# A dense layer with squared ReLU: the four weight chunks of the opening stage on one column half before the other, and the requests reordered to match

## The chip, the cores and the metric

The kernel runs on one core of one Trainium2 chip. Its time is the device time in microseconds, the median of several runs. TensorE multiplies, VectorE and ScalarE copy and apply the activation, SyncE and ScalarE issue the transfers from memory.

## What is computed

```python
B, S, D, F = 1, 2048, 576, 4608          # bf16
h = einsum("bsd,df->bsf", x, w1) + b1
h = relu(h) ** 2
out = einsum("bsf,fd->bsd", h, w2) + b2
```

The inner dimension of the first product is D = 576 = 4 x 128 + 64. The kernel walks over x in four blocks of 512 rows, and over the 4608 columns of w1 in 36 tiles of 128.

## The kernel before

The first product needs x transposed. For blocks 1 to 3 a transposing transfer does it. For block 0, which cannot wait for that, x comes as it is, in four row tiles of 128 rows (`xs`), and TensorE transposes it by chunks of 128 columns. Column half 0 of the transposed block holds row tiles 0 and 1, half 1 holds row tiles 2 and 3. The first four column tiles of w1 (`qn`, "natural" chunks: 128 rows of w1 by 512 columns each) are used with 128-row matmuls, so that TensorE has something to do with few bytes landed. All other columns of w1 are laid out in 64-row pieces (`w1h`, two column tiles to a pair) and are multiplied with pairs of 64-row matmuls.

The requests, in the order of the program; the two issuing queues work side by side, each in its own order:

```python
    load_x(nc.sync, 0)
    load_x(nc.scalar, 1)
    load_quad(nc.sync, 0)
    load_quad(nc.scalar, 1)
    load_x(nc.sync, 2)
    load_x(nc.scalar, 3)
    load_quad(nc.sync, 2)
    load_quad(nc.scalar, 3)
    # ... one dummy activation
    for h in range(2):
        load_rest(nc.sync, h)           # last 64 rows of w1, 512 columns

    for j0, n in ((2, 1), (3, 1), (4, 1), (5, 1), (6, 2), (8, 2), (10, 2), (12, 2), (14, 2), (16, 2)):
        for h in range(2):
            load_w1(nc.sync, h, j0, n, slice(0, NH))     # n pairs from pair j0
```

The two helpers of the opening stage: transposes of some chunks of one half, each followed by a copy out of PSUM on the engine named (V for VectorE, A for ScalarE; chunk NC is the odd rest and takes two copies); and the four matmuls of one chunk on one half.

```python
    def transpose_chunks(half, cs, engs):
        tps = [psum.tile([P, HALF], BF16, name="tp", tag="bank") for c in cs]
        for i in range(2):
            for c, tp in zip(cs, tps):
                d0 = c * P if c < NC else D - P
                nc.tensor.transpose(tp[:, i * P:(i + 1) * P], xs[:, 2 * half + i, d0:d0 + P], ident[:])   # L167
        cols = slice(half * HALF, (half + 1) * HALF)
        for c, tp, eng in zip(cs, tps, engs):
            copy_psum(eng, xT[0][:, c if c < NC else 7, cols], tp[:])            # L160 VectorE, L158 ScalarE
            if c == NC:
                nc.vector.tensor_copy(out=xT[0][0:H, 8, cols], in_=tp[H:P, :])

    def full_mm(half, c):
        cols = slice(half * HALF, (half + 1) * HALF)
        for q in range(4):
            nc.tensor.matmul(bk0[q][:, cols], lhsT=qn[:, c, q * P:(q + 1) * P], rhs=xT[0][:, c, cols], ...)   # L213
```

And the stage itself, in TensorE's order:

```python
    transpose_chunks(0, (0,), (V,))
    transpose_chunks(0, (1,), (A,))
    fill(HALF)
    full_mm(0, 0)
    transpose_chunks(0, (2, NC), (A, V))
    full_mm(0, 1)
    transpose_chunks(0, (3,), (A,))
    transpose_chunks(1, (0, 1, 2), (V, A, V))
    full_mm(1, 0)
    transpose_chunks(1, (NC,), (V,))
    full_mm(1, 1)
    transpose_chunks(1, (3,), (A,))
    full_mm(0, 2)
    full_mm(1, 2)
    # ... transpose of the bias to b1T (L232)
    full_mm(0, 3)
    full_mm(1, 3)
    # ... four matmuls with the last 64 rows (L239), evacuation of the four banks
```

After it come the pairs 2 to 17 of block 0 (`a_step`, 18 matmuls of 64 rows by 512 columns to a pair, L198), then blocks 1 to 3 with all pairs, then the second product (L302, L316).

Of the kernel before, what the change touches and what calls it, by code (L numbers as in the profile page):

```python
# [17 lines left out]
def kernel(  # L18
# [9 lines left out]
    nc = tc.nc  # L28
# [10 lines left out]
    NC = D // P  # L39
# [51 lines left out]
    def load_x(eng, j):  # L91
        eng.dma_start(out=xs[:, j, :], in_=x_view[:, j, :])  # L92

    def load_quad(eng, c):
        eng.dma_start(out=qn[:, c, :], in_=w1[c * P:(c + 1) * P, 0:G * P])  # L95

    def load_w1(eng, h, j0, n, cs):
        f0 = pairs[j0][h] * P
        eng.dma_start(out=w1h[h * H:(h + 1) * H, cs, j0 * P:(j0 + n) * P], in_=w1_rows[:, cs, f0:f0 + n * P])
# [7 lines left out]
    load_x(nc.scalar, 1)  # L107
    load_quad(nc.sync, 0)
    load_quad(nc.scalar, 1)
    load_x(nc.sync, 2)  # L110
    load_x(nc.scalar, 3)
    load_quad(nc.sync, 2)
    load_quad(nc.scalar, 3)
    nc.scalar.activation(out=warm[:], in_=nc.const_aps.tensor(1.0, [P, 1], FP32), func=ACT.Relu)
    for h in range(2):
        load_rest(nc.sync, h)


    for j0, n in ((2, 1), (3, 1), (4, 1), (5, 1), (6, 2), (8, 2), (10, 2), (12, 2), (14, 2), (16, 2)):
        for h in range(2):  # L120
            load_w1(nc.sync, h, j0, n, slice(0, NH))

# [33 lines left out]
    def copy_psum(eng, dst, src):  # L156
        if eng is nc.scalar:
            nc.scalar.copy(out=dst, in_=src)  # L158
        else:
            nc.vector.tensor_copy(out=dst, in_=src)  # L160
# [9 lines that stand above are left out]
            copy_psum(eng, xT[0][:, c if c < NC else 7, cols], tp[:])  # L170
            if c == NC:
                nc.vector.tensor_copy(out=xT[0][0:H, 8, cols], in_=tp[H:P, :])
# [37 lines left out]
# [3 lines that stand above are left out]
            nc.tensor.matmul(bk0[q][:, cols], lhsT=qn[:, c, q * P:(q + 1) * P], rhs=xT[0][:, c, cols],  # L213
                             start=(half == 0 and c == 0), stop=False, skip_group_check=True)

    V, A = nc.vector, nc.scalar
# [4 lines left out]
    transpose_chunks(0, (2, NC), (A, V))  # L221
    full_mm(0, 1)
    transpose_chunks(0, (3,), (A,))
    transpose_chunks(1, (0, 1, 2), (V, A, V))
    full_mm(1, 0)
    transpose_chunks(1, (NC,), (V,))
    full_mm(1, 1)
    transpose_chunks(1, (3,), (A,))
    full_mm(0, 2)
    full_mm(1, 2)  # L230
    b1T_ps = psum.tile([P, P], BF16, name="b1T_ps", tag="bank")
    nc.tensor.transpose(b1T_ps[:], b1_rows[:], ident[:])  # L232
    nc.vector.tensor_copy(out=b1T[:], in_=b1T_ps[:, 0:NFT])
    full_mm(0, 3)
    full_mm(1, 3)
    for i in range(2):
        for h in range(2):
# [118 lines left out]
```

## Time and profile before

| what | value |
|---|---|
| time, median of 3 runs | 291.2 us (290.83 to 291.26) |
| span of the profiled execution | 289.1 us |
| granted TensorE clock, mean | 1.0 of full speed |
| first transpose on TensorE | 2.87 us |
| first pair (L198) on TensorE | 9.76 us |
| w1 pairs, 22 loads by SyncE | 3.3 to 7.8 us from issue to landing |

The profile is of one execution. Its times start at the span's beginning. PE is TensorE's matmuls, PEld its weight loads, DVE is VectorE, ACT is ScalarE; SPq and ACTq are the queues in which SyncE and ScalarE issue transfers. A line such as L167 is a line of the kernel. In the names of the program, `w_sb` covers the several buffers that share the later home of w2: xs, the transposed x and the natural chunks of w1 among them; x is told from w1 there by what is read, `in_x_dram` or `in_w_dram`.

### The profile page before, as it was taken

The page shows a single profiled execution, that of the slowest core. Times are in us where ns is not written, and L with a number is a line of the kernel's source. Part 1 is how long each engine was busy: PE and PEld are TensorE (multiplying, and loading weights), DVE is VectorE, ACT ScalarE, POOL GpSimd, SP SyncE. Part 2 cuts the span into 40 slices and gives each one's busy share as a digit, 9 for nine tenths or more (in the row PEclk, how much of TensorE's full clock was granted, in tenths as well). Part 3 has the DMA queues.
Part 4 walks back from the last instruction along what each step waited for, and adds up shares of the span by engine and source line. Part 5 has one row for each costly group of instructions (what it writes and reads, how often), then busy time and mean ns, then how long its engine had stood idle before and what let it go on. Part 6 is the DMA issues. An engine that isn't in the chain of part 4 may idle for free.

```text
span 289.1 us, 4823 instructions
## 1 busy us (share of the span) xinstructions
PE 284.3 (98%) x2068; PEld 133.3 (46%) x2079; DVE 79.2 (27%) x195; ACT 95.4 (33%) x153; POOL 1.5 (1%) x8
## 2 busy tenths in 40 slices
PE   8999999999999999999999999999999999999995
PEld 5544444444444444444445444444444444444454
DVE  2644454444445444444420011111100011111111
ACT  3666666666666666666620000000000000000000
POOL 2000000000000000000000000000000000000000
PEclk9999999999999999999999999999999999999999
DMA  7999998800300006100000100000000000000000
GB/s 202 210 232 197 212 184 195 299 0 2 120 5 2 1 2 207 40 0 2 0 2 19 20 20 20 20 23 11 10 20 23 20 20 20 24 20 20 20 23 20
DMA packets 35413, 18.01 MB, mean 62 GB/s; under 512 B 19380, under 2 KB 35392, under 8 KB 35392
## 3 DMA queue, kind: packets, MB, share of 16 engines
q1 hardware_dynamic: 34784, 17.14, 25.5%
q10 hardware_dynamic: 576, 0.56, 0.6%
q8 instruction: 16, 0.26, 0.4%
q14 instruction: 5, 0.04, 0.0%
q0 software_dynamic: 32, 0.01, 0.0%
HBM read 11.94 MB, written 2.36 MB: 49 GB/s over the span
## 4 chain that ended last, share of the span: by engine, by line
PE 97%; DMA 2%; issue 0%; SPq 0%; DVE 0%
PE ph L198 47%; PE po L316 43%; PE pc L302 5%; DMA w_sb<-in_x_dram 2%; PE ph L213 1%; PE tp L167 0%; PE ph L239 0%; SPq L95 0%; SPq L92 0%; DVE w_sb L160 0%; DVE o_sb L318 0%; PE b1T_ps L232 0%; SPq L340 0%
## 5 line engine op out<-in xcount | busy, mean ns | idle before, releaser
L182 ACT ACTIVATE r<-ph,b1T 128x512 bf16<-128x512 f32 x144 | 90.8, 684 | 48.4 <-PE ph L198 46.6
L198 PE MATMUL ph<-w_sb,w1h 64*128 64x512 bf16 x936 | 101.2, 376 | 0.0
L198 PEld LDWEIGHTS <-w1h 64*128 64x128 bf16 x1260 | 61.3, 94 | 74.7
L316 PE MATMUL po<-w_sb,hT 128*128 128x512 bf16 x423 | 92.9, 379 | 0.5
L316 PEld LDWEIGHTS <-hT 128*128 128x128 bf16 x432 | 42.2, 98 | 51.1 <-issue 0.4
L184 DVE TENSOR_TENSOR hT<-r 128x512 bf16<-128x512 bf16 x108 | 45.9, 425 | 54.8 <-ACT r L182 54.1
L318 DVE TENSOR_TENSOR o_sb<-po,b_bc 128x512 bf16<-128x512 f32 (+2 forms) x17 | 11.2, 660 | 116.7 <-PE po L316 109.7
L198 PE MATMUL ph<-xT,w1h 64*128 64x512 bf16 x324 | 35.1, 376 | 0.0
L316 PE MATMUL po<-w_sb,w1h 128*128 128x512 bf16 (+2 forms) x178 | 31.2, 336 | 0.1
L316 PEld LDWEIGHTS <-w1h 128*128 128x128 bf16 x180 | 16.2, 98 | 15.3
L184 DVE TENSOR_TENSOR w1h<-r 128x512 bf16<-128x512 bf16 x36 | 15.3, 425 | 19.7 <-ACT r L182 19.5
L302 PE MATMUL pc<-hT,w_sb 128*64 128x512 bf16 x108 | 15.7, 379 | 0.0
L302 PEld LDWEIGHTS <-w_sb 128*64 128x64 bf16 x144 | 8.1, 110 | 7.6 <-issue 0.4
L302 PE MATMUL pc<-w1h,w_sb 128*64 128x512 bf16 x36 | 7.9, 379 | 0.0
L304 ACT ACTIVATE oc<-pc,b2T 128x512 bf16<-128x512 f32 x2 | 1.4, 687 | 13.7 <-PE pc L302 13.7
L312 DVE COPY o_sb<-oc 128x64 bf16<-128x64 bf16 x16 | 2.7, 171 | 9.3 <-DMA oc<-oc 9.3
L213 PE MATMUL ph<-w_sb 128*128 128x256 bf16 x32 | 4.5, 283 | 0.3 <-DVE w_sb L160 0.3
L213 PEld LDWEIGHTS <-w_sb 128*128 128x128 bf16 x32 | 3.1, 103 | 1.0 <-issue 0.6
L150 PE MATMUL wps<-const-bfloat16-1.0 128*128 128x512 bf16 x5 | 2.3, 624 | 0.8 <-PEq L340 0.8
L160 DVE COPY w_sb<-tp 128x256 bf16<-128x256 bf16 x5 | 1.4, 289 | 5.7 <-PE tp L167 5.7
L158 ACT COPY w_sb<-tp 128x256 bf16<-128x256 bf16 x5 | 1.8, 368 | 2.6 <-PE tp L167 2.6
L167 PE MATMUL tp<-ident,w_sb 128*128 128x128 bf16 x20 | 2.5, 239 | 0.1
(28 smaller groups left out, 11.2 us busy)
## 6 DMA issues: line engine op xcount, KB each, us to landing
w_sb<-in_w_dram SPq DMA_DIRECT2D x6, 864.0 KB, 7.1
w1h<-in_w_dram SPq DMA_DIRECT2D x14, 288.0 KB, 7.1
out_dram<-o_sb SPq DMA_DIRECT2D x15, 144.0 KB, 1.7
w1h<-in_w_dram SPq DMA_DIRECT2D x8, 144.0 KB, 3.6
w_sb<-in_x_dram SPq DMA_DIRECT2D x2, 144.0 KB, 3.3
w_sb<-in_x_dram ACTq DMA_DIRECT2D x2, 144.0 KB, 3.5
w_sb<-in_w_dram SPq DMA_DIRECT2D x2, 128.0 KB, 3.7
w_sb<-in_w_dram ACTq DMA_DIRECT2D x2, 128.0 KB, 3.9
```

What stands on the lines that cost most here:

```text
L150: nc.tensor.matmul(wps[:], lhsT=ones[:, 0:P], rhs=ones[:], start=(i == 0), stop=(i == NWARM - 1))
L158: nc.scalar.copy(out=dst, in_=src)
L160: nc.vector.tensor_copy(out=dst, in_=src)
L167: nc.tensor.transpose(tp[:, i * P:(i + 1) * P], xs[:, 2 * half + i, d0:d0 + P], ident[:])
L182: nc.scalar.activation(out=r[:], in_=bk[:], func=ACT.Relu, bias=b1T[:, ft:ft + 1], scale=1.0)
L184: nc.vector.tensor_tensor(out=hT_of(b, ft), in0=r3, in1=r3, op=ALU.mult)
L198: nc.tensor.matmul(bk[h][:], lhsT=w1h[rows, c, j * P:(j + 1) * P], rhs=xT[b][rows, place(h, c), :], start=(i == 0), stop=(i == NH - 1))
L213: nc.tensor.matmul(bk0[q][:, cols], lhsT=qn[:, c, q * P:(q + 1) * P], rhs=xT[0][:, c, cols], start=(half == 0 and c == 0), stop=False, ski ...
L302: nc.tensor.matmul(pc[h * H:(h + 1) * H, :], lhsT=w2(ft, DM, D), rhs=hT_of(2 * pr + h, ft), start=(ft == 0), stop=(ft == NFT - 1))
L312: nc.vector.tensor_copy(out=o_sb[:, DM:D], in_=o_tr[pr][:, jj, h * H:(h + 1) * H])
L316: nc.tensor.matmul(po[:, 0:e - a], lhsT=hT_of(b, ft)[:, jj, :], rhs=w2(ft, a, e), start=(ft == 0), stop=(ft == NFT - 1))
L318: nc.vector.tensor_tensor(out=o_sb[:, a:e], in0=po[:, 0:e - a], in1=b2_bc[:, a:e], op=ALU.add)
```

## The change

The stage is put in another order. All four natural chunks run on column half 0 before the stage turns to half 1, so that TensorE has the work of chunk 2 while it waits for row tiles 2 and 3 of x. For that, w1 chunk 2 is requested ahead of x's third row tile (third in SyncE's queue), that row tile goes to ScalarE's queue, the fourth row tile comes fourth in SyncE's queue, and chunk 3 is requested behind it, fourth in ScalarE's. Half 1 is transposed in three portions in place of one of three chunks and two of one, and its last copy moves from ScalarE to VectorE. Beside that, the last two w1 loads of two pairs for each 64-row half become one of four pairs.

```diff
     load_quad(nc.sync, 0)
     load_quad(nc.scalar, 1)
-    load_x(nc.sync, 2)
-    load_x(nc.scalar, 3)
     load_quad(nc.sync, 2)
+    load_x(nc.scalar, 2)
+    load_x(nc.sync, 3)
     load_quad(nc.scalar, 3)
...
-    for j0, n in ((2, 1), (3, 1), (4, 1), (5, 1), (6, 2), (8, 2), (10, 2), (12, 2), (14, 2), (16, 2)):
+    for j0, n in ((2, 1), (3, 1), (4, 1), (5, 1), (6, 2), (8, 2), (10, 2), (12, 2), (14, 4)):
         for h in range(2):
             load_w1(nc.sync, h, j0, n, slice(0, NH))
...
     transpose_chunks(0, (3,), (A,))
-    transpose_chunks(1, (0, 1, 2), (V, A, V))
+    full_mm(0, 2)
+    transpose_chunks(1, (0, 1), (V, A))
+    full_mm(0, 3)
+    transpose_chunks(1, (2, NC), (A, V))
     full_mm(1, 0)
-    transpose_chunks(1, (NC,), (V,))
+    transpose_chunks(1, (3,), (V,))
     full_mm(1, 1)
-    transpose_chunks(1, (3,), (A,))
-    full_mm(0, 2)
-    full_mm(1, 2)
     # ... transpose of the bias (L232) and its copy
-    full_mm(0, 3)
+    full_mm(1, 2)
     full_mm(1, 3)
```

## The prediction

> **What bounds the kernel now.** I read the page's busy shares first, then the chain of work that ended last in order of time, then the timeline of the first ten microseconds, and last the transfers' times to landing, asked for one narrow stretch of issue times after another. The busy line says that TensorE leaves no room, and the chain says where the little room is.
>
> ```profile
> PE 284.3 (98%) x2068; PEld 133.3 (46%) x2079; DVE 79.2 (27%) x195; ACT 95.4 (33%) x153; POOL 1.5 (1%) x8
> ```
>
> ```profile
> 0.99 4.40 DMA w_sb<-in_x_dram
> 5.39 0.05 issue
> 5.44 0.52 PE tp L167 x4
> 5.96 0.02 issue
> 5.98 0.30 DVE w_sb L160
> 6.29 0.04 issue
> 6.33 0.60 PE ph L213 x4
> 6.92 0.11 PE tp L167 x2
> 7.04 0.44 PE ph L213 x4
> 7.47 0.11 PE tp L167 x2
> 7.58 0.87 PE ph L213 x8
> 8.46 0.06 PE b1T_ps L232
> 8.51 0.87 PE ph L213 x8
> 9.39 0.54 PE ph L239 x4
> 9.93 135.97 PE ph L198 x1260
> ```
>
> Columns are start, length, and what ran. From 9.93 us on the chain is TensorE alone, 1260 matmuls in one piece (135.97 / 1260 = 108 ns each), and the rest of the 289.1 us span follows them without a wait worth naming. The change touches nothing there but the size of two loads. So all that can move is the stretch before, where the chain goes through x's row tile 2 (requested at 0.99, landed at 5.39), the transposes of row tiles 2 and 3, one VectorE copy, and then 3.06 us of TensorE work from 6.33 to 9.39.
>
> The four transfers that the change permutes, by the timeline (start, length, issuing queue) and by the issue view (KB, us from issue to landing):
>
> ```profile
> 0.99 0.43 SPq L92 DMA_DIRECT2D w_sb<-in_x_dram  x1
> 1.10 0.45 ACTq L92 DMA_DIRECT2D w_sb<-in_x_dram  x1
> 1.47 0.43 SPq L95 DMA_DIRECT2D w_sb<-in_w_dram  x1
> 1.58 0.45 ACTq L95 DMA_DIRECT2D w_sb<-in_w_dram  x1
> ```
>
> ```profile
> w_sb<-in_x_dram SPq DMA_DIRECT2D x1, 144.0 KB, 4.4
> w_sb<-in_x_dram ACTq DMA_DIRECT2D x1, 144.0 KB, 4.6
> w_sb<-in_w_dram SPq DMA_DIRECT2D x1, 128.0 KB, 4.8
> w_sb<-in_w_dram ACTq DMA_DIRECT2D x1, 128.0 KB, 4.9
> ```
>
> Adding them: row tile 2 lands at 5.39, row tile 3 at 5.70, w1 chunk 2 at 6.27, chunk 3 at 6.48. TensorE agrees: its weight loads for the transposes resume at 5.44 and at 5.71, right behind the landings. TensorE is thus idle from about 5.13 (the last transpose of the first half issued at 5.02 and 5.07) to 5.44, nearly from 5.55 to 5.71, and from 5.87 to 6.33. That is 0.9 us, and the change is aimed at it.
>
> [...] a transfer's landing depends more on its place in its queue than on what it carries. The trace agrees: first requests land at 2.4 and 2.7 us, second at 3.1 and 3.6, third at 5.4 and 5.7, fourth at 6.3 and 6.5, always the pair of both queues together. [...] by the byte rates in slices of 0.15 us, all 1.11 MB of the eight transfers have moved by about 5.1 us if nothing else is counted, more than a microsecond before the last landing. [...] The gaps of up to half a microsecond here did not do it (the matmuls after 6.33 keep 0.11 us), and I expect no longer ones after the change.
>
> **The change, part by part.** It adds and removes no arithmetic: 4160 TensorE rows before and after.
>
> First, the requests. SyncE's queue becomes row tile 0, chunk 0, chunk 2, row tile 3; ScalarE's becomes row tile 1, chunk 1, row tile 2, chunk 3. Each queue still carries 2 x 144 + 2 x 128 KB. By place in the queue: chunk 2 at about 5.39 (its place carries 16 KB less, so perhaps 5.3), row tile 2 at 5.70, row tile 3 at 6.27 (16 KB more, perhaps 6.3), chunk 3 at 6.48. What is won is chunk 2 (0.9 us earlier); what is paid is row tile 3 (0.57 later) and row tile 2 (0.31 later).
>
> Second, TensorE's order. Until 5.13 nothing changes. Then: the four matmuls of chunk 2 on the first half wait for chunk 2: 5.43 to 5.87 (4 x 0.11). The two transposes of row tile 2 follow to 5.98. The two of row tile 3 wait for it: 6.31 to 6.42. The four matmuls of chunk 3 on the first half wait for chunk 3: 6.48 + 0.04 = 6.52. From there TensorE should run dense. Durations from the starts in the timeline: 0.44 (chunk 3, first half) + 0.22 (four transposes) + 0.44 (chunk 0, second half) + 0.11 (two transposes) + 0.44 (chunk 1) + 0.06 (the bias transpose) + 0.97 (chunks 2 and 3 with the change to 64-row matmuls, which the timeline has from 8.35 to 9.32) = 2.68 us. So the last four matmuls of this stage (L239) start at 6.52 + 2.68 = 9.20, where the timeline of before has 9.32. **Gain 0.12 us.** Before, the stretch after the last wait was 9.32 - 6.33 = 2.99: the change moves one group (0.44) ahead of the last wait and puts two transposes (0.11) behind it, less 0.02 of rounding, so 0.31 shorter; but the last wait ends 0.19 later, 6.52 against 6.33, because it is now the last transfer of all rather than the third pair with a copy.
>
> Third, the copies. Chunk 0's second half is copied after row tile 3's transposes, 6.31 + 0.06 + 0.22 latency, so from 6.6 to 6.9 (0.29 on VectorE); its matmuls start at 6.52 + 0.66 = 7.18. Chunk 1's copy on ScalarE ends at 7.05 (0.37), needed at 7.73. The copy of chunk 3, now VectorE's and behind the two copies of the odd rest, ends near 8.3, needed at 8.67. None is on the path; the first has 0.3 us of slack.
>
> Fourth, w1's columns. The loads of 2 + 2 pairs become one of 4 (two instructions instead of four, same bytes, runs twice as long). TensorE needs pair 14 at 9.93 + 12 x 1.94 = 33.2 us (18 matmuls of 108 ns to a pair). In the rates of the first 30 us the w1 stream falls off at about 28 us, and the last request has 7.7 us to landing from 21.7. Even if pair 14 now comes with the very last byte, at about 29.5, 3.7 us are left. Worth 0.
>
> Sum: 291.2 - 0.1 = **291.1 us**.
>
> **Rivals.** (a) *The late row tile is the new bound.* Row tile 3 now rides in the last place; if its landing is 0.3 later than reckoned (6.6 rather than 6.27), the first-half matmuls of chunk 3 stand behind its transposes in TensorE's order and the stage starts at 6.75: 291.3, slower by 0.1. For it: 16 KB more and SyncE's short loads right behind. Against: both queues carry the same bytes as before. (b) *The pairs of landings are not set by place but by what is carried* (the x rows took longer than the weights, 1152-byte rows against 1024). Then chunk 2 could land near 5.0 and the last pair with it a little earlier; TensorE waits less, and 0.2 to 0.4 us come off: 290.9. Against: the first pair is x too and landed quickest. (c) *The joined load is late.* If a load of four pairs is slower to complete, or the transposing loads behind it are issued earlier and compete, pair 14 waits and up to 1 to 2 us are lost, 292 to 293. Against: 3.7 us of slack, and before, the transposing loads moved nothing until the w1 stream had drained (rates of 55 and 14 GB/s just ahead of 29 us). (d) *A gain of the whole 0.9 us* of idle time would need the last transfer to land by 5.7; nothing in the change makes a transfer faster as a whole. Chance below one in twenty.
>
> **Range and chances.** The three runs of before lie within 0.43 us, more than the effect. The landings can shift 0.3 us either way. I take 290.7 to 291.5 for 8 in 10. Two per cent is 5.8 us; the whole stage touched is under 10 us long, most of it work that stays, so a gain of 2% is excluded by arithmetic, and a loss of 2% needs a failure that I do not see: 0.005 faster, 0.985 within, 0.01 slower.
>
> **What will show it.** Right: the chain of after enters TensorE from a landing at 6.3 to 6.5 instead of 5.39 and passes through no copy; chunk 2 is awaited near 5.4; L239 starts near 9.2; the piece of 1260 matmuls is whole and as long as before. Wrong: a gap inside the 1260 matmuls (c); L239 later than 9.32 with a wait on x (a); L239 before 9.0 with chunk 3 landed before 6.3 (b); or a copy as the last wait ahead of chunk 0's second half, which would mean that my slack of 0.3 us was misjudged.

## The result, and the profile after

| | time, median | lowest to highest | runs |
|---|---|---|---|
| before | 291.08 us | 290.83 to 291.43 | 6 |
| after | 290.17 us | 289.91 to 290.84 | 6 |

The ratio is 0.9972, 95% interval 0.9958 to 0.9985. The change gains about 0.9 us here, where 0.1 was predicted; two later comparisons give 0.9971 and 0.9979, by their medians 0.7 and 0.5 us. 290.17 lies below the range of 290.7 to 291.5. Within 2% was right, the size was not.

The first surprise is in the profile. The profiled execution of after has a span of 289.1 us, exactly that of before, although the spans of the five other runs are 288.1 to 288.7. It is the slowest of the six, so it has to be read for what binds, not for the gain. From the page, the busy line (the PEld share of 65% is of this one profile; the two later profiles of after have 46%, as before has):

```profile
PE 285.0 (99%) x2068; PEld 187.6 (65%) x2079; DVE 79.3 (27%) x195; ACT 95.5 (33%) x153; POOL 1.5 (1%) x8
```

And the chain of work that ended last, in order of time (start, length, what ran), for the same stretch that was shown of before:

```profile
0.78 2.29 PE wps L150 x5
3.08 0.43 PE tp L167 x4
3.50 0.21 PE wps L153
3.71 0.97 PE ph L213 x4
4.68 0.43 PE tp L167 x4
5.11 0.85 PE ph L213 x4
5.96 0.21 PE tp L167 x2
6.17 0.56 PE ph L213 x4
6.73 0.22 PE tp L167 x4
6.96 0.44 PE ph L213 x4
7.39 0.22 PE tp L167 x4
...
9.53 0.54 PE ph L239 x4
10.07 136.07 PE ph L198 x1260
```

Two things are to be seen. There is no transfer and no copy in it: from the first warming matmul on, TensorE follows TensorE. And the same group of four L213 matmuls takes 0.85 us at 5.11 but 0.44 at 6.96; four transposes take 0.43 at 4.68 and 0.22 at 6.73. TensorE ran at half its clock until somewhere past 6 us (the page's clock line shows nine tenths or more all along; the trace's record of the full clock begins at 6.3 us). In the profile of before the groups of four take 0.44 from 4.58 on, and the record begins at 4.2.

The four permuted transfers of after, by the issue view over narrow stretches (KB, us from issue to landing); they were issued at 0.99 (chunk 2), 1.09 (row tile 2), 1.47 (row tile 3) and 1.58 (chunk 3):

```profile
w_sb<-in_w_dram SPq DMA_DIRECT2D x1, 128.0 KB, 3.7
w_sb<-in_x_dram ACTq DMA_DIRECT2D x1, 144.0 KB, 3.8
w_sb<-in_x_dram SPq DMA_DIRECT2D x1, 144.0 KB, 3.8
w_sb<-in_w_dram ACTq DMA_DIRECT2D x1, 128.0 KB, 4.0
```

So they landed at 4.7, 4.9, 5.3 and 5.6 us, where I had reckoned with 5.4, 5.7, 6.3 and 6.5. Three questions follow: is the earlier landing due to the new order of requests or to chance, does the moment of the full clock depend on the kernel, and what is it that the change really removes?

### The profile page after: what moved, and what is told of

It is laid out like the page before. It is cut to its first block, busy times and chain, and to the rows that moved or that the text cites. A ratio compares the mean times of both kernels' runs of the same rounds, so it can differ in the third digit from the quotient of the medians.

```text
span 289.1 us, 4821 instructions
## 1 busy us (share of the span) xinstructions
PE 285.0 (99%) x2068; PEld 187.6 (65%) x2079; DVE 79.3 (27%) x195; ACT 95.5 (33%) x153; POOL 1.5 (1%) x8
## 4 chain that ended last, share of the span: by engine, by line
PE 99%; issue 0%; DVE 0%
PE ph L198 47%; PE po L316 43%; PE pc L302 5%; PE ph L213 2%; PE wps L150 1%; PE tp L167 1%; PE ph L239 0%; DVE o_sb L318 0%; PE wps L153 0%; PE b1T_ps L232 0%
## 5 line engine op out<-in xcount | busy, mean ns | idle before, releaser
L198 PEld LDWEIGHTS <-w1h 64*128 64x128 bf16 x1260 | 115.0, 94 | 21.1 <-DMA w1h<-in_w_dram 0.2
L213 PE MATMUL ph<-w_sb 128*128 128x256 bf16 x32 | 5.5, 314 | 0.0
L213 PEld LDWEIGHTS <-w_sb 128*128 128x128 bf16 x32 | 3.3, 112 | 0.7 <-DMA w_sb<-in_w_dram 0.2
L160 DVE COPY w_sb<-tp 128x256 bf16<-128x256 bf16 x5 | 1.5, 291 | 6.5 <-PE tp L167 6.5
L167 PE MATMUL tp<-ident,w_sb 128*128 128x128 bf16 x20 | 2.7, 265 | 0.0
L167 PEld LDWEIGHTS <-w_sb 128*128 128x128 bf16 x20 | 2.1, 122 | 0.9 <-DMA w_sb<-in_x_dram 0.6
```

The source lines that it names most:

```text
L198: nc.tensor.matmul(bk[h][:], lhsT=w1h[rows, c, j * P:(j + 1) * P], rhs=xT[b][rows, place(h, c), :], start=(i == 0), stop=(i == NH - 1))
```

## The experiments

Every profile below has its own landings and its own clock. This table gathers them, in us: landings in the order in which the queues carry them (third places, then fourth), the moment at which the trace's record of the full clock begins, and the start of L239 in the chain.

| profile | third places | fourth places | full clock | L239 |
|---|---|---|---|---|
| before | 5.39, 5.67 | 6.22, 6.44 | 4.2 | 9.39 |
| before again (e1) | 5.16, 5.53 | 5.88, 6.06 | 4.9 | 9.47 |
| joined load only (e6) | 5.22, 5.67 | 5.95, 6.13 | 5.4 | 9.52 |
| requests only (e3) | 5.19, 5.52 | 5.95, 6.15 | 4.3 | 9.66 |
| order only (e4) | 4.34, 5.12 | 5.56, 5.76 | 6.4 | 9.63 |
| after | 4.70, 4.88 | 5.30, 5.56 | 6.3 | 9.53 |
| after again (e2) | 5.41, 5.63 | 6.05, 6.25 | 6.2 | 9.50 |
| after, third time (e9) | 4.67, 5.18 | 5.47, 5.62 | 6.4 | 9.57 |
| after, split load (e5) | 5.11, 5.50 | 5.87, 6.04 | 5.9 | 9.34 |
| after, split load again (e10) | 5.26, 5.62 | 5.96, 6.13 | 4.4 | 8.93 |

### Both kernels once more

No edit. The kernel before:

> The kernel before, unchanged, profiled once more. Theory P (the request order decides: a row tile of x in third place on both queues is slow): row tiles 2 and 3 land again at 5.3 to 5.8 us, chunks 2 and 3 at 6.2 to 6.5; time 291.1, ratio 1.000. Theory R (the landings of one execution are chance): the four landings differ from the first profile by 0.5 us or more. In either case the moment at which TensorE gets its full clock (4.2 us in the first profile) may differ by up to 3 us.

The changed kernel:

> The changed kernel, unchanged, profiled once more. P: the four transfers land again at 4.6 to 5.7 us and TensorE waits for none; if the full clock comes by 4.5 us the four matmuls L239 start at 8.5 to 8.7 and the span is 288.1 to 288.4; if it comes near 6.3 us, 9.4 to 9.5 and 289.1. Time 290.2, ratio 0.997. R: the landings fall back to 5.4 to 6.5, and the span is then 288.9 or more even with an early clock.

Before: 291.16 us, ratio 1.000 (0.9991 to 1.0009). After: 290.30 us, ratio 0.9971 (0.9958 to 0.9983). The gain is real. The early landings, though, were chance: the same two kernels now land in third and fourth place at nearly the same times as each other, 5.2 to 6.1 before and 5.4 to 6.3 after. Theory P, that the order of the requests makes the transfers quicker, falls. The place in the queue decides, as predicted (SyncE's third transfer lands at 5.03 on the mean of four profiles as row tile 2, and at 5.06 on the mean of six as chunk 2); but one and the same place varies by 0.8 to 1.1 us over the ten profiles. The second profile of after has landings within 0.25 us of the ones I had reckoned with, and still its chain contains no transfer: with the clock full only at 6.2, TensorE got to each piece after it had landed.

Whether the clock depends on the kernel, no run decides. In the table the four profiles with the old order of TensorE have it full by 5.4, and five of the six with the new order only from 5.9. But TensorE runs the same instructions in both until after 5 us, and in the pairs with more warming below it came at 4.25, 3.41 and 6.01 with the old order (e11, e13, e7) and at 6.03 and 3.50 with the new (e12, e8). What the table does show is what a late clock costs: in the old order L239 moves by 0.13 as the clock moves from 4.2 to 5.4, in the new one by 0.41 from 4.4 to 5.9.

### The requests alone, TensorE's order alone

```diff
-    load_x(nc.sync, 2)
-    load_x(nc.scalar, 3)
     load_quad(nc.sync, 2)
+    load_x(nc.scalar, 2)
+    load_x(nc.sync, 3)
     load_quad(nc.scalar, 3)
```

> The request order of after, TensorE's order and the w1 loads of before. P: the landings are those of after (last row tile at about 5.3 rather than 5.7), so TensorE's transposes of row tile 3 come 0.4 us earlier and the time falls by 0.3 to 0.5: ratio 0.9985, half of the gain. R: the order of the requests is nothing in itself, row tile 3 is now in the last place and lands at about 6.3: slower by 0.5, ratio 1.002. If the TensorE order alone carries the gain: ratio 1.000 to 1.002.

291.09 us, ratio 0.9998 (0.9989 to 1.0008). Nothing is gained and nothing clearly lost. Its chain does go through the row tile that now rides last, and through the copy behind its transposes:

```profile
1.47 4.48 DMA w_sb<-in_x_dram
5.95 0.05 issue
5.99 0.24 PE tp L167
6.24 0.02 issue
6.26 0.30 DVE w_sb L160
```

The other half: the new order of TensorE with the requests and loads of before.

```diff
     transpose_chunks(0, (3,), (A,))
-    transpose_chunks(1, (0, 1, 2), (V, A, V))
+    full_mm(0, 2)
+    transpose_chunks(1, (0, 1), (V, A))
+    full_mm(0, 3)
+    transpose_chunks(1, (2, NC), (A, V))
     full_mm(1, 0)
-    transpose_chunks(1, (NC,), (V,))
+    transpose_chunks(1, (3,), (V,))
     ...   # and the rest of TensorE's order as in the changed kernel
```

> TensorE's order of after, requests and w1 loads of before. P: chunk 2 lands fourth, at 6.3, and stands ahead of row tile 2's transposes in TensorE's order, so TensorE waits from 5.1 to 6.3 and the matmuls L239 start at 6.3 + 3.1 = 9.4: 291.1 to 291.4, ratio 1.000 to 1.001. R and 'the order alone carries the gain': 290.2 to 290.4, ratio 0.997 to 0.998.

290.83 us, ratio 0.9988 (0.9978 to 0.9999): between the two expectations. Its profile happens to have the earliest row tiles of all and a late clock, so chunk 2, landed at 5.56, held TensorE up for 0.2 us at most. The order of TensorE carries something by itself. It falls 0.5 us short of the changed kernel, but that has the joined load too; against the changed kernel without it (0.9991 and 0.9984, next section) nothing is missing that is clear of noise. So what the new requests are worth with the new order is not shown.

### The joined load

```diff
-    for j0, n in (..., (12, 2), (14, 4)):
+    for j0, n in (..., (12, 2), (14, 2), (16, 2)):
```

> The changed kernel with the last w1 loads of before (2 + 2 pairs rather than 4). If the joined load has no part in the gain: 290.2 to 290.4, ratio 0.997 as with it. If the joined load carries part: 290.6 or more. In its profile, whichever moment the clock becomes full, the four matmuls L239 start no later than 9.65 us, as TensorE is its own bound.

The reverse, the join alone in the kernel before:

> The kernel before with the joined w1 load alone. No part: ratio 1.000 (0.999 to 1.001), 291.0. Part: 0.9985 or less. The 1260 matmuls of L198 stay one piece of 136.0 us in either case.

Split in the changed kernel: 290.64 us, ratio 0.9991 (0.9982 to 1.0000), which looked as if the join were worth 0.3 us or more. Alone: 290.81 us, ratio 1.0004 (0.9990 to 1.0017), nothing. The two seem to disagree (though the second interval reaches down to 0.9990), so both forms of the changed kernel were run once more, side by side on one chip:

> The changed kernel once more, beside the same with the split load on the same chip. If the joined load carries part of the gain: again 0.9971 and at least 0.3 us below the split one. If the difference between the two earlier results (0.9971 with the joined load, 0.9991 with the split one) was chance of landings and clock: both within 0.2 us of each other, near 0.998.

> The changed kernel with the last w1 loads of before, once more. Joined load carries part: 0.9985 to 0.9995, 0.3 us or more above the joined one. Chance: within 0.2 us of it. The joined load is issued after 17 us, so no event ahead of 10 us should differ in either case.

290.48 us each: 0.9979 (0.9970 to 0.9988) joined, 0.9984 (0.9978 to 0.9991) split. By these times alone the first difference looks like chance. Over all runs the joined form has a median of 290.37 (46 runs), the split one of 290.61 (35 runs on other chips in part).

The profiles show that the load does carry a part, at the end of the program and not where its bytes are used. There SyncE waits for its transfers by six waits, one after another in a fixed order, among them that for the landing of the last store. The wait for that landing, in e10 (split) and then in e9 (joined), from the view of SyncE's waits (us in total, times, longest; L351 is the line that ends the program):

```profile
SPq L351 <- DMA out_dram<-o_sb: 1.1, 1, 1.1
```

```profile
SPq L351 <- DMA out_dram<-o_sb: 0.8, 1, 0.8
```

| last w1 loads | profiles | wait for the last store | its landing to the end of the program |
|---|---|---|---|
| 2 + 2 pairs | before, e1, e3, e4, e5, e10, e11, e13, e14 | second of six | 1.12 us |
| one of 4 pairs | after, e2, e6, e9, e12, e15 | last of six | 0.89 to 0.90 us |

In all of them the last store lands 1.53 to 1.54 us after VectorE's last instruction. But behind the second wait four more follow, of 0.06 us each, although what they wait for is long done; where the wait is the last, they have been passed while the store was under way. In the traces of before and after the landings are counted on eight counters in turn (nine transfers on each of two counters and eight on each of six in before, eight on each of the eight in after; the one transfer that GpSimd issues has its own), so the number of transfers decides which wait the last store falls to: there are 67 with the two loads and 65 with the joined one. The late pair below (e7 and e8) has four more of them each, and there the store has moved on: to the fourth wait in e7 (71 transfers, 1.01 us from its landing to the end), to the second in e8 (69, 1.15 us). So the joined load is worth **0.22 us**, in the kernel before as in the changed one. It fits the medians of 290.37 and 290.61; in a single comparison it is of the size of the interval.

The split profile of e10 is the one that caught an early clock in the new order, and its chain shows the change at work:

```profile
4.84 0.44 PE ph L213 x4
5.28 0.11 PE tp L167 x2
5.39 0.52 PE ph L213 x4
5.92 0.37 PE tp L167 x4
6.29 0.50 PE ph L213 x4
...
8.93 0.54 PE ph L239 x4
```

Chunk 2, the transposes and chunk 3 follow each other with 0.08, 0.15 and 0.06 us lost (0.52, 0.37 and 0.50 against 0.44, 0.22 and 0.44). Weight loads of TensorE do wait for transfers here (0.3 us for chunk 2, the longest), so some of this is the price that was predicted. L239 starts at 8.93, where before with a like clock had 9.39.

### Transfers made to bind: a pair that missed its aim

```diff
+    for k in range(4):
+        (nc.sync, nc.scalar)[k % 2].dma_start(
+            out=hT[2][:, 4 * k:4 * k + 4, :],
+            in_=w1[k * P:(k + 1) * P, 0:4 * SB].rearrange("p (a s) -> p a s", s=SB))
     load_x(nc.sync, 0)
     ...
-    NWARM = 5
+    NWARM = 20
```

Four further loads ahead of all others, on both kernels:

> The kernel before with four further loads of 512 KB each ahead of its first requests (into a buffer that is written anew later, so nothing that is computed changes) and 20 warming matmuls rather than 5. The transfers now come some 6 us later and find TensorE at full clock: the stage is bound by transfers alone, as the prediction's sum supposed. About 297 us; TensorE idle between the row tiles by 1 us or more.

> The changed kernel with the same four loads ahead and 20 warming matmuls. Theory W (the change removes waits for transfers, whatever the clock): 0.6 to 1.0 us faster than the other late kernel. Theory C (the sum of the prediction holds where transfers alone bind, and what came on top is from executions in which the clock came late and the work, not the transfers, was the bound): 0.1 to 0.3 us faster than the other late kernel.

295.89 us and 296.41 us (ratios to the kernel before 1.0172, 1.0157 to 1.0186, and 1.0175, 1.0156 to 1.0193). As a test of the two theories it is void. In the first the eight transfers of the stage came so close behind each other (the row tiles of half 1 had landed by 9.89 us, all eight by 10.57) that TensorE, which began its transposes at 8.33 and turned to half 1 after 10.35, met no wait for them there. In the second the clock had become full early, at 3.5 us, the warming matmuls were done at 6.6, TensorE waited 2.11 us for the first row tiles, and the clock went back to half. Its chain (the added lines shift the numbers: L217 here is L213 elsewhere, L171 is L167):

```profile
9.58 0.60 PE ph L217 x4
10.18 0.22 PE tp L171 x4
10.40 0.85 PE ph L217 x4
...
13.95 0.44 PE ph L217 x4
```

But the first of the two left a number that asked for more: with no transfer late at the half and the clock full (from 6.0), TensorE still took 6.00 us from the first transpose (8.33) to L239 (14.33), and had an idle stretch of 0.27 ahead of chunk 0 on half 1, behind a VectorE copy.

### Everything landed, full clock: the stage by itself

```diff
-    NWARM = 5
+    NWARM = 22
```

On both kernels, so that neither a transfer nor the clock is left in the stage:

> The kernel before with 22 warming matmuls rather than 5: all eight transfers have landed and the clock is full before the first transpose. TensorE's stage then takes 6.0 us from the first transpose to L239 (as it did behind the late transfers, 8.33 to 14.33), one copy wait of 0.27 included. About 295 us.

> The changed kernel with 22 warming matmuls. If the change gains by waits for transfers alone: only the copy wait goes, 0.2 to 0.4 us faster than the other warmed kernel, 5.7 us from the first transpose to L239. If something else in the change gains (the joined load, later stages): 0.8 us or more faster, as without the warming.

The times, 294.97 and 294.56 us (1.0138, 1.0125 to 1.0152, and 1.0117, 1.0102 to 1.0131, to the kernel before), contain warming of a length that depends on the clock (the 22 warming matmuls take 6.64 us in e11, full clock at 4.25, and 7.51 us in e12, full clock at 6.03); the stage itself is to be read in TensorE's timeline. Warmed, before:

```profile
7.26 0.38 PE L167 MATMUL tp<-ident,w_sb 128*128 128x128 bf16 x4
...
9.01 0.82 PE L167 MATMUL tp<-ident,w_sb 128*128 128x128 bf16 x8
10.10 0.60 PE L213 MATMUL ph<-w_sb 128*128 128x256 bf16 x4 [0.27 <-DVE w_sb L160]
...
13.09 0.61 PE L239 MATMUL ph<-w_sb 64*128 64x512 bf16 x4
```

Warmed, after:

```profile
8.13 0.38 PE L167 MATMUL tp<-ident,w_sb 128*128 128x128 bf16 x4
...
9.88 0.28 PE L167 MATMUL tp<-ident,w_sb 128*128 128x128 bf16 x2
10.01 0.60 PE L213 MATMUL ph<-w_sb 128*128 128x256 bf16 x4
...
13.33 0.60 PE L239 MATMUL ph<-w_sb 64*128 64x512 bf16 x4
```

From the first transpose to L239: 5.83 us before, 5.20 after. The change is worth **0.63 us in this stage with no transfer to wait for**, twice the 0.31 that I had allowed. From the first transpose to the end of the program it is 285.57 against 284.72 (the spans of 292.83 and 292.85 less 7.26 and 8.13), so 0.85: the 0.63 and the 0.22 of the joined load. In the plain kernels the stage gains less (e10 shows 0.29 us lost between its pieces): the changed kernel with the split load lies 0.35 to 0.38 us below before (290.61 against 290.96 and 290.99 on the same chips), e10 by its L239 0.46. The place is the turn to half 1. Before, eight transposes (the last of half 0 and six of half 1) need 8 x 0.055 = 0.44 us, but from the first of them (9.01) to the next matmul (10.10) pass 1.09: 0.65 us are idle. The waits of TensorE's weight loads name the first part of it:

```profile
PEld L167 <- DVE w_sb L172: 0.2, 1, 0.2
```

The transpose of the third chunk needs a PSUM slot that the second copy of the odd rest (L172) has yet to free. Then chunk 0's last transpose has to run to its end and be copied before the first matmul on half 1 (in the chain of e11 the transposes end at 9.73, the VectorE copy runs from 9.75 to 10.05, the matmuls start at 10.10), and nothing else stands in TensorE's order for that time.

### The turn taken apart

Two edits of the warmed kernel before. In the first, two chunks are transposed at the turn rather than three, and the third goes with the odd rest:

```diff
-    transpose_chunks(1, (0, 1, 2), (V, A, V))
+    transpose_chunks(1, (0, 1), (V, A))
     full_mm(1, 0)
-    transpose_chunks(1, (NC,), (V,))
+    transpose_chunks(1, (2, NC), (A, V))
```

> The warmed kernel before, with two chunks of half 1 transposed at the turn rather than three, the third with the odd rest. Theory B (the gain is the bubble at the turn: slot wait 0.2 us, then copy latency 0.45): the slot wait goes, 5.6 to 5.7 us from the first transpose to L239. If the bubble is no part of it: 5.8.

In the second, nothing but four independent matmuls moves:

```diff
     transpose_chunks(1, (0, 1, 2), (V, A, V))
+    full_mm(0, 2)
     full_mm(1, 0)
     ...
     transpose_chunks(1, (3,), (A,))
-    full_mm(0, 2)
     full_mm(1, 2)
```

> The warmed kernel before, with nothing but the four matmuls of chunk 2 on half 0 moved ahead of those of chunk 0 on half 1. Theory B: they fill the copy's latency, 5.4 us from the first transpose to L239 (0.43 less), the slot wait stays. If the bubble is no part: 5.8.

TensorE's timeline of the first (294.97 us, ratio 1.0140, 1.0122 to 1.0158):

```profile
6.85 0.38 PE L167 MATMUL tp<-ident,w_sb 128*128 128x128 bf16 x4
...
8.60 0.50 PE L167 MATMUL tp<-ident,w_sb 128*128 128x128 bf16 x6
9.43 0.60 PE L213 MATMUL ph<-w_sb 128*128 128x256 bf16 x4 [0.33 <-DVE w_sb L160]
...
12.53 0.61 PE L239 MATMUL ph<-w_sb 64*128 64x512 bf16 x4
```

And of the second (294.40 us, ratio 1.0113, 1.0098 to 1.0127):

```profile
7.51 0.39 PE L167 MATMUL tp<-ident,w_sb 128*128 128x128 bf16 x4
...
9.26 0.82 PE L167 MATMUL tp<-ident,w_sb 128*128 128x128 bf16 x8
9.91 1.04 PE L213 MATMUL ph<-w_sb 128*128 128x256 bf16 x8
...
12.90 0.61 PE L239 MATMUL ph<-w_sb 64*128 64x512 bf16 x4
```

12.53 - 6.85 = 5.68 (5.6 to 5.7 expected) and 12.90 - 7.51 = 5.39 (5.4 expected). So the four matmuls of chunk 2 in the copy's shadow are worth 0.44 of the 0.63, and the smaller portions, which have no wait for a slot, make up the other 0.19 by subtraction; the 0.15 that they bring alone is of that size, but the two were not run together without the rest of the change. What the change gains in the stage is this bubble, idle time of TensorE in the middle of its work.

### One warming matmul fewer

```diff
-    NWARM = 5
+    NWARM = 4
```

On the changed kernel, as its chain begins with the five warming matmuls:

> The changed kernel with 4 warming matmuls rather than 5. If TensorE's own work is the bound from its first matmul on: the transposes start at 2.9 behind row tile 1 rather than at 3.1, and 0.1 to 0.25 us are gained, 290.2, ratio 0.9972. If the clock comes later for the gap of 0.2 us, or the transfers bind after all: 290.4 to 290.8.

290.47 us, ratio 0.9982 (0.9972 to 0.9991): no gain. Row tile 1 landed at 2.98 in this profile, and the transposes waited for it until 3.03, so the warming matmul had cost 0.05 us at most.

## Why the prediction was wrong, point by point

- **The step that failed** is the last wait of the second part, "The four matmuls of chunk 3 on the first half wait for chunk 3: 6.48 + 0.04 = 6.52", with the term built on it, "the last wait ends 0.19 later". The shortening of 0.31 behind the wait was real; the price was not paid. With the clock early (e10) chunk 3 landed at 6.13, its matmuls start at 6.29, 0.04 earlier than the 6.33 of before, and L239 comes 2.64 behind that. The 0.19 came from one profile: there chunk 3 landed 0.77 behind row tile 3, the widest gap between the third and the fourth transfer of ScalarE's queue in the ten profiles (0.44 to 0.77, mean 0.58). An estimate with the mean: the wait now ends 0.58 + 0.04 behind the third landing, where before it ended 6.33 - 5.67 = 0.66 behind it, so 0.04 earlier; with the 0.31 the stage gains 0.35, about what the split form shows. With the clock late no transfer stands in the chain: in the three profiles of after chunk 3 landed at 5.56, 6.25 and 5.62, and TensorE, at half clock until 6.2 to 6.4, reached its matmuls only at 6.9 to 7.0.
- **The second failed term** is the fourth part, "Worth 0". The pairs came in time, as reckoned there, but two transfers fewer move the wait for the last store at the program's end, 0.22 us.
- **What was read too narrowly** is the idle time of before. The sum has 5.87 to 6.33 as a part of the wait for the third pair of landings. It is the turn's own bubble: 0.65 us in the warmed kernel, where everything has landed. The lines were in my own fence: "5.98 0.30 DVE w_sb L160" stands between two pieces of TensorE in the chain, and in the warmed kernel, whose data had come early, TensorE stands idle at the same copy. In the second profile of before the row tiles landed 0.14 to 0.23 us earlier, the same copy stands in the chain, and L239 is no earlier; but its clock came 0.65 us later too, so the warmed pair, not this, is the proof.
- **What was taken as constant and is not**: the landings, from one profile, which turned out to be the latest of the ten in the fourth places; and the clock. Of the clock I asked only whether gaps of up to half a microsecond bring it down to half; that the sum rests on a full clock from 4.2 us on, the record of one profile, I did not say. Over the profiles the record of the full clock begins between 3.4 us (e13) and 6.5 us (e15) after the start, and at 4.2 and 4.9 us in two profiles of one and the same kernel (before and e1). I should have spread the sum over that.
- **Right**: landings go by place in the queue and not by content, now on ten profiles (SyncE's third place: 5.03 us on the mean with x, 5.06 with w1); no arithmetic added (2079 weight loads in both traces; the "4160 TensorE rows" stand in neither); the 2.68 us of dense TensorE from chunk 3 on (8.93 - 6.29 = 2.64 in e10, 9.53 - 6.96 = 2.57 in after); the copies of half 1 off the path (in after none is in the chain, as predicted); the 1260 matmuls in one piece, 135.97 us in most profiles and 136.07 in the first of after, with one wait of 0.2 us for a w1 pair near 17.9 us, which is not the joined one.
- **Rivals**: (a) did not occur in after, though e3 shows its wait with the order of before. (b) gave 290.9 and is the nearest in number, but for a cause that fell: what is carried does not set the landing. (c) did not occur. (d), which I gave less than one in twenty, came true in size in the first comparison (0.9), not in the later two (0.7 and 0.5), by a way that I had not listed: part of the idle time needs no earlier transfer, and 0.22 us lie at the other end of the program.
- **The marks**: that the chain passes through no copy was met, and was the one that mattered; "enters TensorE from a landing at 6.3 to 6.5" and "L239 starts near 9.2" were not.

One thing stays open: how bubble, clock and landings mix in a plain run. The runs without a profile don't show their landings or clock, and the three profiles of after are all among its slower executions (290.84, 290.72 and 290.78 us against medians of 290.17, 290.30 and 290.48). In them L239 is no earlier than before (9.50 to 9.57 against 9.39 to 9.52); the gain in the stage is seen in e10 and in the warmed pair, and in the times. Before was not profiled with a clock later than 5.4, so what the change gains there is not shown.

## What to carry to other kernels

A copy or a wait for a slot between two pieces of the bottleneck engine in the chain is a bubble of its own (0.65 us in e11), even when a late transfer stands just ahead of it; put independent work of that engine into it, and reckon this gain apart from that of the transfers. A change in the number of transfers can move the end of a program without touching any work (0.22 us between 67 and 65 transfers): compare what follows the last store's landing. In the first ten microseconds one profile is one draw: landings moved by up to 1.1 us (SyncE's third place, 4.34 to 5.41) and the clock by 3 us (3.4 to 6.5) between executions, so a sum from one profile needs a spread for both. And when a changed kernel's profile shows the old span while its runs are faster, look first at whether TensorE's groups take double time in its opening (0.85 us for four matmuls against 0.44 in after).

## What was not expected of the hardware

The granted clock fell back after an idle time of about two microseconds: in e8 TensorE was idle for 2.11 us (6.62 to 8.73) and lightly used just after, and from 10.3 to 13.7 us the matmuls took twice their time (0.85 per group of four against 0.44). Gaps of up to half a microsecond in the other profiles did no such thing (0.49 us ahead of the first transpose in e7, where a group of four still takes 0.43 to 0.44 behind it). And the clock line of the page of after reads nine tenths or more through the opening in which the groups show half rate (0.85 us at 5.11 against 0.44 at 6.96): there the length of a group of equal matmuls is the better clock. And a wait on a transfer that has long landed is not free: each took SyncE about 0.06 us at the end of the program (from 287.99 to 288.24 us four of them in before).
